# The queue of the first head's second load, and the place of one VectorE piece ahead of the first row maximum

## The chip, the cores and the metric

One core of a Trainium2 chip runs the whole program. The metric is the time that the device needs for one execution, in microseconds (us); of several runs the median counts.

## The reference

An attention with hashed buckets for 4 batches of 8 heads (768 tokens, 64 dimensions a head), followed by a mixture of 8 experts with one expert a token.

```python
q_bits = (np.einsum('bhsd,dk->bhsk', q, proj) > 0).astype(np.int64)
k_bits = (np.einsum('bhsd,dk->bhsk', k, proj) > 0).astype(np.int64)
powers = 2 ** np.arange(n_bits)
q_bucket = np.sum(q_bits * powers, axis=-1)
k_bucket = np.sum(k_bits * powers, axis=-1)
mask = q_bucket[:, :, :, None] == k_bucket[:, :, None, :]
scores = scale * np.matmul(q, k.transpose(0, 1, 3, 2))
scores = np.where(mask, scores, -1000000000.0)
scores = scores - np.max(scores, axis=-1, keepdims=True)
attn = np.exp(scores)
attn = attn / (np.sum(attn, axis=-1, keepdims=True) + 1e-09)
return np.matmul(attn, v).astype(np.float32)
...
for e in range(E):
    lo, hi = (boundaries[e], boundaries[e + 1])
    if lo == hi:
        continue
    h = np.maximum(x_sorted[lo:hi] @ w1[e], 0.0)
    y_sorted[lo:hi] = h @ w2[e]
y = y_sorted[inv_perm]
return (gate_w[:, None] * y).astype(np.float32)
```

## The kernel before

The 32 heads go in 16 pairs. A head's scores are made in units of 128 queries by 768 keys (12 units a pair), each in one of three PSUM buffers: two matmuls of the rounded halves of q and k (L309) and two of what rounding left, together with rows that hold the hash bits as large numbers (L307), so that keys of another bucket fall out in the exponent. VectorE takes a unit's row extreme and copies the unit to SBUF (L319, `peak`, called the maximum here), ScalarE takes the exponent (L325), and TensorE transposes (L339) and multiplies by v. Later pairs are transposed on VectorE and by DMA; the mixture of experts follows from about the middle of the run.

The order of the work on all engines is written out by hand. HEAD, a list of words, holds the first pair's order; `step` turns each word into instructions, and every engine executes its own in the order of the list. A word's first letter is the step, then come a head and a half (of 384 tokens), and a last letter names the engine (A ScalarE, V VectorE, P GpSimd). For the first pair:

- `load_first(h)` (L72 to L77) loads head h: the k half of the tile (columns S to 2S) first, then the q half, 384 KB each, both issued on SyncE (L76). L89 loads pj, the 16 KB of hash directions, on ScalarE's queue.
- k, j, q, l and p (`cut`, L219 to L236) make the parts of `qk` from the loaded tile `xd`: k and q round (L232 on ScalarE, L234 and L236 elsewhere), j takes what k's rounding left (L228, VectorE, needs k of the same half and the k load), l the same for q (L230), p copies q (L232, L236).
- y (L242) multiplies the loaded tile by pj; y01 takes the k load, y00 the q load. y11 and y10 are those of the second head.
- b (`bits_first`) turns y's result into bits: halves 0 and 1 on VectorE (L253), 2 and 3 on ScalarE (L247). b12 and b13 write over rows that j10V and j11V wrote.
- i are warming matmuls (L104), as are ten at the start.
- f0 and f1 are the two parts of the scores of unit 0; S1, S2, S11 and so on the scores of those units, R0, R1 their maxima (L319), X0, X1 their exponents (L325).
- G multiplies the next pair's tile by pj (L264), in a PSUM buffer that b12 and b13 have read before; H takes the signs of it.

ScalarE's pieces from k01A on are k01A, q00A, p00A, b03, b02, k11A, k10A, p10A, q10A, b13, b12, X0. GpSimd's are p01P, q01P, l01P, p11P, q11P, l11P, l10P. VectorE's are shown below under the change.

Of the kernel before, what the change touches and what calls it, by code (L numbers as in the profile page):

```python
# [15 lines left out]
B, H, S, D = 4, 8, 768, 64  # L16
# [38 lines left out]
def lsh_attention_moe(ctx, tc, qk, qk2, v, proj, wg, w1, w1p, w2, w2p, out):  # L55
    nc = tc.nc
# [15 lines left out]
    def load_first(h):  # L72

        x = wk.tile([128, 2 * S], F32, name="xd")
        for c in ((S, 2 * S), (0, S)):
            nc.sync.dma_start(x[:, c[0]:c[1]], qk2[h][:, c[0]:c[1]])  # L76
        XD[h] = x  # L77

    def load_pair(g):
# [3 lines left out]
    def load_v(g):  # L83
        VT[g] = wk.tile([128, NT, 2, D], F32, name="vt", bufs=3)
        nc.sync.dma_start(VT[g], v[g])

    load_first(0)
    pj = const.tile([128, 32], F32, name="pj")
    nc.scalar.dma_start(pj, proj)  # L89
    load_first(1)  # L90
    small = const.tile([128, 1], F32, name="small")
    nc.gpsimd.memset(small, -TINY)
# [928 lines left out]
    def weight_half(op, x):  # L1021
# [18 lines left out]
    lows = []  # L1040

    HEAD = """
        k01A k00V j00V y01 q00A j01V p00A y00 l00V b03 b00 i02 f0 p01P b02 q01P b01 k11A i12 f1 k10A j11V y11 R0 j10V
        y10 p10A q10A b13 l01P b12 S1 X0 p11P b11 b10 S2 G H R1 X1 R2 X2 q11P l11P S11 R11 X11 S10 R10 X10 l10P S4 T01
        E01v T00 E00v S5 T02 E02a S9 T51 E51a R5 X5 R4 X4 T50 E50v T52 E52a R9 X9 S3 R3 X3 S8 T20 E20v T21 E21v s01 w
        S7 T22 E22a R8 T10 E10a X8 A1 R7 X7 S6 s11 s13 s03 T11 E11v T12 E12v T41 z0 E41v R6 T40 e E40a T42 E42v z1 A2 s00
# [309 lines left out]
```

## Time and profile before

| | us |
|---|---|
| median of 3 runs | 679.37 |
| lowest and highest run | 679.32, 1693.6 |
| profiled execution | 679.44 |
| its span, first to last instruction | 677.7 |

The granted clock of TensorE is 1.0 of full speed in the profiled execution. In the rows of the profile PE is TensorE's matmuls, PEld its weight loads, DVE VectorE, ACT ScalarE, POOL GpSimd, SP SyncE; a q behind the name (SPq, ACTq) is the engine's sequencer, which issues DMAs. L76 is line 76 of the kernel.

### The profile page before, as it was taken

What the parts mean: (1) busy time and instruction counts of PE and PEld (TensorE: products, weight loads), DVE (VectorE), ACT (ScalarE), POOL (GpSimd) and SP (SyncE); (2) the same over time, 40 slices, a digit from 0 to 9 for tenths busy, and PEclk for the clock granted to TensorE, in tenths of its full rate; (3) what the DMA queues carried; (4) which work ended last, traced back from release to release, by engine and by line L of the source; (5) the groups of instructions that cost most, each with busy time, mean ns of one, the idle gap of its engine ahead of it and who ended that gap; (6) DMA issues with size and microseconds to landing.
All of it is one profiled execution on the core that took longest, in us unless ns stands there. A gap on an engine that the chain in (4) does not pass through costs nothing.

```text
span 677.7 us, 12615 instructions
## 1 busy us (share of the span) xinstructions
PE 666.5 (98%) x4359; PEld 564.1 (83%) x4359; DVE 471.2 (70%) x879; ACT 409.7 (60%) x816; POOL 468.0 (69%) x524
## 2 busy tenths in 40 slices
PE   8999999999999999999999999999999999999997
PEld 4777887788777887787777878899999999989896
DVE  8999889988899889998985555351453635463661
ACT  7977887788878887787765225453444444434310
POOL 7878666977797778877864636845476685959622
PEclk9999999999999999999999999999999999999999
DMA  7689999899889788997885358656648484857202
GB/s 278 210 248 291 254 264 278 211 255 238 228 238 263 197 239 238 261 246 192 242 250 162 116 199 243 158 183 159 168 150 218 147 214 145 227 190 226 96 10 43
DMA packets 74321, 138.51 MB, mean 204 GB/s; under 512 B 16609, under 2 KB 37345, under 8 KB 74256
## 3 DMA queue, kind: packets, MB, share of 16 engines
q1 hardware_dynamic: 66528, 118.57, 61.7%
q0 software_dynamic: 7584, 19.10, 9.5%
q8 instruction: 35, 0.57, 0.4%
q14 instruction: 30, 0.25, 0.2%
q10 hardware_dynamic: 144, 0.02, 0.0%
HBM read 63.39 MB, written 26.33 MB: 132 GB/s over the span
## 4 chain that ended last, share of the span: by engine, by line
PE 93%; ACT 2%; DVE 2%; issue 1%; DMA 1%; SPq 0%; POOL 0%; POOLq 0%; ACTq 0%; DVEq 0%
PE s L888 22%; PE t L415 12%; PE s L927 11%; PE s L961 10%; PE s L307 10%; PE s L309 9%; PE t L429 7%; PE t L339 7%; PE t L470 3%; PE t L264 2%; PE t L104 1%; ACT e L325 1%; DMA pt<-w 1%; ACT qk L215 0%; SPq L383 0%
## 5 line engine op out<-in xcount | busy, mean ns | idle before, releaser
L325 ACT ACTIVATE e<-e,m 128x768 f32<-128x768 f32 x192 | 178.3, 930 | 37.5 <-DVE e L319 36.0
L319 DVE TENSOR_SCALAR_CACHE_REDUCE e<-s 128x768 f32<-128x768 f32 x192 | 176.3, 951 | 25.3 <-PE s L309 20.2
L784 POOL TENSOR_TENSOR w<-raw,w 128x512 fp32r<-128x512 f32 x112 | 142.4, 1299 | 33.2 <-ACT w L783 32.3
L888 PE MATMUL s<-xh,w 128*128 128x456 f32 (+6 forms) x672 | 123.9, 345 | 0.0
L888 PEld LDWEIGHTS s<-xh,w 128*128 128x128 f32 x672 | 120.0, 188 | 3.1
L904 DVE SCALAR_TENSOR_TENSOR hh<-s,hh 128x256 fp32r<-128x256 f32 (+7 forms) x64 | 35.5, 555 | 86.8 <-ACT hh L902 86.7
L376 DVE STREAM_TRANSPOSE z<-e 128x1536 f32<-128x1536 f32 x52 | 90.7, 1763 | 2.3 <-DMA pt<-z 1.2
L415 PE MATMUL t<-pt,vt 128*64 128x256 f32 x720 | 81.0, 381 | 0.0
L902 ACT ACTIVATE hh<-s 128x256 fp32r<-128x256 f32 (+7 forms) x64 | 31.4, 491 | 80.8 <-PE s L888 80.8
L927 PE MATMUL s<-hh,w 128*128 128x456 f32 (+3 forms) x384 | 74.7, 355 | 0.0
L927 PEld LDWEIGHTS s<-hh,w 128*128 128x128 f32 x384 | 71.3, 188 | 2.7
L415 PEld LDWEIGHTS t<-pt,vt 128*64 128x64 f32 x720 | 50.4, 137 | 27.6 <-issue 3.1
L339 PE MATMUL t<-ident,e 128*128 128x128 f32 x468 | 68.9, 277 | 2.8 <-DVE pt L404 1.7
L339 PEld LDWEIGHTS t<-ident,e 128*128 128x128 f32 x468 | 53.3, 140 | 20.7 <-ACT pq L406 6.9
L783 ACT ACTIVATE w<-raw 128x512 fp32r<-128x512 f32 x112 | 66.3, 622 | 3.4 <-DMA raw<-in_w1p_dram 3.1
L961 PE MATMUL s<-w,hh 128*128 128x512 f32 (+1 forms) x240 | 56.4, 394 | 0.0
L406 ACT ACTIVATE pq<-t 128x512 f32<-128x512 f32 x83 | 47.8, 591 | 11.6 <-PE t L339 9.9
L307 PE MATMUL s<-w 80*128 80x384 f32 x192 | 54.1, 363 | 0.0
L307 PE MATMUL s<-qk 80*128 80x384 f32 x192 | 53.7, 361 | 0.0
L961 PEld LDWEIGHTS s<-w,hh 128*128 128x128 f32 (+1 forms) x240 | 44.7, 187 | 10.6
L309 PE MATMUL s<-qk 128*128 128x384 f32 x192 | 50.0, 341 | 0.0
L309 PE MATMUL s<-w 128*128 128x384 f32 x192 | 49.7, 340 | 0.0
(236 smaller groups left out, 1046.4 us busy)
## 6 DMA issues: line engine op xcount, KB each, us to landing
pt<-z SPq DMA_DIRECT2D x208, 192.0 KB
raw<-in_w1p_dram SPq DMA_DIRECT2D x28, 512.0 KB
xd<-in_qk_dram SPq DMA_DIRECT2D x14, 768.0 KB
sorted_rows<-xr SPq DMA_DIRECT2D x8, 1156.0 KB
raw<-in_w_dram SPq DMA_DIRECT2D x18, 512.0 KB
raw<-in_w2p_dram SPq DMA_DIRECT2D x16, 512.0 KB
vt<-in_v_dram SPq DMA_DIRECT2D x16, 384.0 KB
masks<-bits POOLq DMA_DIRECT2D x14, 192.0 KB
```

Source lines behind the costliest of these rows:

```text
L307: nc.tensor.matmul(p[:, a, :HALF], k[0:80, 2, c], k[0:80, 3, n], start=i >= 4, stop=i < 4)
L309: nc.tensor.matmul(p[:, a, :HALF], k[:, 0, c], k[:, 1, n], start=i < 4, stop=i >= 4)
L319: nc.vector.tensor_scalar(e, SC.pop(i)[:, :, :HALF], CEIL, None, op0=OP.min, op1=OP.min, accum_out=m)
L325: nc.scalar.activation(e, e, AF.Exp, bias=m, scale=-1.0, accum_out=SM[g][:, 3 * hf + t, s:s + 1])
L339: nc.tensor.transpose(o[:, j, w], e[w][:, kt // 3, (kt % 3) * 128:(kt % 3) * 128 + 128], ident)
L376: nc.vector.transpose(z[:, :, o].rearrange("p g (k i) -> p g k i", i=32), e)
L415: nc.tensor.matmul(PV[u][s * 64:(s + 1) * 64].rearrange("p (t b a i) -> p a t b i", t=4, b=2, a=2)[:, h], VT[g][:, kt, s, :], PT[u][:, h:: ...
L783: nc.scalar.activation(w[:, 0, a], r, AF.Copy)
L784: nc.gpsimd.tensor_tensor(w[:, 1, a], r, w[:, 0, a], op=OP.subtract)
L888: nc.tensor.matmul(p[:, :c], w[:, a, d, fs], x[:, b, d, :c], start=(k == 0), stop=(k == 11))
L927: nc.tensor.matmul(p[:, :c], w[:, a, f % 4, ms], h[b][:, f, :c], start=(k == 0), stop=(k == 23))
L961: nc.tensor.matmul(p[:pw], HH[n][b][:, f, i:i + pw], w[:, a, f % 4], start=(k == 0), stop=(k == 23))
```

## The change

Two edits. In `load_first` the second load (the q half) of head 0 is issued on ScalarE's queue; since `load_first(0)` stands ahead of the load of pj, it comes ahead of pj there. And in HEAD the word j10V stands in front of R0.

```diff
@@ -72,8 +72,8 @@
     def load_first(h):
 
         x = wk.tile([128, 2 * S], F32, name="xd")
-        for c in ((S, 2 * S), (0, S)):
-            nc.sync.dma_start(x[:, c[0]:c[1]], qk2[h][:, c[0]:c[1]])
+        for c, q in ((S, nc.sync), (0, nc.sync if h else nc.scalar)):
+            q.dma_start(x[:, c:c + S], qk2[h][:, c:c + S])
         XD[h] = x
...
     HEAD = """
-        k01A k00V j00V y01 q00A j01V p00A y00 l00V b03 b00 i02 f0 p01P b02 q01P b01 k11A i12 f1 k10A j11V y11 R0 j10V
+        k01A k00V j00V y01 q00A j01V p00A y00 l00V b03 b00 i02 f0 p01P b02 q01P b01 k11A i12 f1 k10A j11V y11 j10V R0
```

On VectorE, from l00V (L230) on, before (the two L253 rows are b00, b01 and b11, b10; L228 is j11V, then j10V; L319 is R0, then R1 and three more):

```order
L230 TENSOR_TENSOR qk<-xd,qk 64x384
L253 TENSOR_SCALAR qk<-t,thr,mul 16x384 x2
L228 SCALAR_TENSOR_TENSOR qk<-xd,qk 80x384
L319 TENSOR_SCALAR e,m<-s 128x768
L228 SCALAR_TENSOR_TENSOR qk<-xd,qk 80x384
L253 TENSOR_SCALAR qk<-t,thr,mul 16x384 x2
L319 TENSOR_SCALAR e,m<-s 128x768 x4
```

The same place now:

```order
L230 TENSOR_TENSOR qk<-xd,qk 64x384
L253 TENSOR_SCALAR qk<-t,thr,mul 16x384 x2
L228 SCALAR_TENSOR_TENSOR qk<-xd,qk 80x384 x2
L319 TENSOR_SCALAR e,m<-s 128x768
L253 TENSOR_SCALAR qk<-t,thr,mul 16x384 x2
L319 TENSOR_SCALAR e,m<-s 128x768 x4
```

j11V and j10V follow each other, and R0 comes behind both; the rest of VectorE's order is as it was.

On ScalarE, at its start, now (before, the row of L76 was not there and pj's stood first):

```order
L76 DMA xd<-in_qk_dram 128x768
L89 DMA pj<-in_proj_dram 128x32
L97 ACT_TABLE_LOAD
L97 ACTIVATE warm<-warm 1x1
L232 ACTIVATE qk<-xd 128x384 x2
L232 ACTIVATE qk<-xd 80x384
```

One issue more stands ahead of pj's. SyncE's row of L76 has three issues where it had four, and all behind it is unchanged, as are TensorE's and GpSimd's orders.

## Rows read from the trace of the kernel before

**Rows 1.** The page: TensorE's busy time, and the chain's shares by engine.

```profile
PE 666.5 (98%) x4359; PEld 564.1 (83%) x4359; DVE 471.2 (70%) x879; ACT 409.7 (60%) x816; POOL 468.0 (69%) x524
...
PE 93%; ACT 2%; DVE 2%; issue 1%; DMA 1%; SPq 0%; POOL 0%; POOLq 0%; ACTq 0%; DVEq 0%
```

**Rows 2.** The chain in order of time (start, length, what), and TensorE's timeline at S2.

```profile
5.38 0.79 PE t L242 x6
...
9.55 1.33 DVE qk L228
...
11.53 0.85 PE t L264 x8
...
10.19 0.52 PE L307 MATMUL s<-qk 80*128 80x384 f32 x2
```

**Rows 3.** Timeline of VectorE: start, length, line, operation, [idle before <-releaser].

```profile
4.52 1.02 DVE L228 SCALAR_TENSOR_TENSOR qk<-xd,qk 80x384 fp32r<-80x384 f32 x2
...
6.40 1.37 DVE L253 TENSOR_SCALAR qk<-t,thr,mul 16x384 fp32r<-16x384 f32 x2
7.99 0.55 DVE L228 SCALAR_TENSOR_TENSOR qk<-xd,qk 80x384 fp32r<-80x384 f32 x1 [0.23 <-ACT qk L232]
8.58 0.96 DVE L319 TENSOR_SCALAR_CACHE_REDUCE e<-s 128x768 f32<-128x768 f32 x1
...
9.46 1.41 DVE L228 SCALAR_TENSOR_TENSOR qk<-xd,qk 80x384 fp32r<-80x384 f32 x1
10.90 1.36 DVE L253 TENSOR_SCALAR qk<-t,thr,mul 16x384 fp32r<-16x384 f32 x2
12.20 0.94 DVE L319 TENSOR_SCALAR_CACHE_REDUCE e<-s 128x768 f32<-128x768 f32 x1
```

**Rows 4.** Waits from 3.5 to 20 us: total, times, longest.

```profile
ACT qk L247 <- DVE qk L228: 1.1, 1, 1.1
...
ACT pq L406 <- PE t L339: 0.5, 1, 0.5
PEld s L307 <- DVE e L319: 0.5, 2, 0.2
```

**Rows 5.** Timeline of the first DMA issues, columns as in rows 3.

```profile
0.77 0.39 ACTq L89 DMA_DIRECT2D pj<-in_proj_dram  x1
0.77 1.84 SPq L76 DMA_DIRECT2D xd<-in_qk_dram  x4
```

**Rows 6.** Timeline of ScalarE and VectorE: their first pieces on the loads.

```profile
4.12 0.52 ACT L232 ACTIVATE qk<-xd 128x384 fp32r<-128x384 f32 x1 [1.43 <-DMA xd<-in_qk_dram]
4.12 0.36 DVE L234 TENSOR_SCALAR qk<-xd 128x384 fp32r<-128x384 f32 x1 [0.84 <-DMA xd<-in_qk_dram]
...
5.09 0.94 ACT L232 ACTIVATE qk<-xd 128x384 fp32r<-128x384 f32 x2 [0.45 <-DMA xd<-in_qk_dram]
...
6.25 1.16 ACT L247 ACTIVATE qk<-t,small 16x384 fp32r<-16x384 f32 x2 [0.22 <-PE t L242]
...
7.44 1.76 ACT L232 ACTIVATE qk<-xd 128x384 fp32r<-128x384 f32 x4
```

**Rows 7.** Two stretches: length, engines' busy time, PEclk, DMA share, GB/s.

```profile
1.50:3.50 2.00, 2.00 (x6) 0.72 (x5) 1.68 (x14) 1.18 (x2) 1.00 (x2) 1.00 0.60 200
3.50:4.50 1.00, 1.00 (x4) 0.32 (x3) 0.36 (x1) 0.38 (x1) 0.20 (x2) 1.00 1.01 402
```

**Rows 8.** DMA queues, whole run, then 1.5 to 2.8 us: packets, MB, share.

```profile
q10 hardware_dynamic: 144, 0.02, 0.0%
...
q1 hardware_dynamic: 34, 0.10, 31.0%
q10 hardware_dynamic: 99, 0.01, 5.7%
```

**Rows 9.** Timeline of GpSimd: the casts of the fourth load, and l11P.

```profile
8.25 1.11 POOL L236 CAST qk<-xd 80x384 fp32r<-80x384 f32 x2 [0.48 <-DMA xd<-in_qk_dram]
9.45 1.01 POOL L230 TENSOR_TENSOR qk<-xd,qk 64x384 fp32r<-64x384 f32 x1
```

## Prediction

> **What bounds the kernel now.** I read the page first. TensorE is busy 666.5 of 677.7 us, and the chain that ended last lies on it for 93% of the span [rows 1]. So the kernel is a row of matmuls in a fixed order, and anything that delays or advances TensorE near the start moves the end by as much, unless slack further on takes it up. The change touches only the first 13 us, so I followed the chain through those, in order of time [rows 2]. The reader is to see that there it is not TensorE alone: after the ten warming matmuls end at 5.39 it goes through the two small matmul groups of L242, a few ScalarE pieces, then VectorE to 10.88 (9.55 + 1.33), one ScalarE sign and the matmuls of L264 at 11.53. Behind it stand score groups on TensorE, but these go in VectorE's step: the waits of the stretch show weight loads of L307 that stood twice, 0.5 us in all, for VectorE's L319 [rows 4], that is, for a maximum to free a PSUM buffer. So what counts is the time at which VectorE begins the second maximum, R1: 12.20 [rows 3].
>
> VectorE itself has hardly a hole from 4.12 to there [rows 3]: k00V, j00V, j01V, l00V, b00, b01, then 0.23 us of waiting for ScalarE, j11V at 7.99, R0 at 8.58, j10V at 9.46, b11 and b10 from 10.90, R1 at 12.20. One piece stands out. The pieces of L228 are the same operation on 80 x 384 elements; j11V takes 0.55 us and j10V 1.41.
>
> **Part 1, the queue of the first head's second load.** Removed: one of four issues at L76 on SyncE, which take 1.84 us for four, 0.46 each. Added: one on ScalarE's queue, ahead of the 0.39 us issue of pj [rows 5]. ScalarE's start-up work moves back by about 0.46; it stood idle for 1.43 us in front of its first piece at 4.12 [rows 6], which hides that. The SyncE DMAs behind are issued 0.46 earlier, but their data wait in the same stream behind the first loads; the issue itself costs and saves nothing.
>
> What matters is the arrival. ScalarE's k01A and VectorE's k00V both start at 4.12, when the first load (the k half of head 0) is there; q00A starts at 5.09 when the second is there, about one load later [rows 6]. The DMA engines move 200 GB/s from 1.5 to 3.5 and 402 GB/s from 3.5 to 4.5 [rows 7], that is 400 KB by 3.5 and 802 KB by 4.5. The first load (128 x 768 x 4 bytes = 393 KB) and pj (16) are 409 KB, reached at 3.52, and the release came 0.60 later; with the second load it is 802 KB, reached at 4.50, released 0.59 later. After 3.5 the transfers are bound by the engines' rate (share 1.01), not by the issue. A second queue therefore brings no earlier second load; the question is only how the two queues share. The packets of pj, the one transfer on ScalarE's queue now, answer it in part: that queue, q10, carries 144 packets in the whole run, and from 1.5 to 2.8 us 99 of them moved while SyncE's q1 moved 34 [rows 8]. Neither queue waited for the other to drain. If they share so with two loads of equal packets, each gets half, both are moved at 786 KB, reached at 4.46, and both land near 5.05, the first perhaps a packet earlier. Bounds for the delay of the first load: 0 (served as now) and 0.97 (landing with the second, 5.09 - 4.12). I take 0.90, 5.02 for the first load, near the upper end, because the packet counts are the nearest row.
>
> The Trainium skill speaks against this part: the page "DMA: Bandwidth & Descriptors", section "Rules for kernel authors", says that spreading DMAs over several issuing engines brings no bandwidth, since they run on the same 16 DMA engines and interleave, and its section "Queues, rings and completion order" that each engine goes round its queues packet by packet. The packet counts of rows 8 agree with it. By the rule alone the sum takes the upper bound, without it the lower.
>
> pj now comes behind the second load in ScalarE's queue, so after about 4.46 + 0.6 = 5.06, beside packets of the third load; it landed early enough in the trace for L242 to start right behind the warming matmuls. I put it between 5.1 and 5.7 (0.60 for the last part, and up to 0.6 of sharing), so TensorE waits 0 to 0.3 us at L242. That is covered: b03 on ScalarE needs the first half of L242 (half of its 0.79 us [rows 2]) and also VectorE's j01V, which now ends at 4.52 + 1.02 = 5.54 [rows 3] and with the later load at 6.44. Only a pj after about 6.0 would cost anything.
>
> Now VectorE with the first load at 5.02: the pieces up to b01 ended at 7.77 and end at 8.67. The 0.23 us of waiting for k11A in front of j11V goes: on ScalarE k01A runs 5.02 to 5.54, q00A and p00A to 6.50, b03 and b02 (1.16) to 7.67, k11A to about 8.2, so it is ready. j11V starts at 8.69, 0.70 late. On TensorE f1, y11, y10, S1 and S2 move by no more than the 0.90 of the load. S2 ended at 10.71 [rows 2] and so ends at 11.6 at the latest, with S1 0.9 ahead of it, before R1 (12.0) and R2 need them.
>
> **Part 2, j10V ahead of R0.** Nothing is added; two neighbours on VectorE change places. j10V needs k10A (ScalarE's four pieces from 7.44 end at 9.20 in the trace [rows 6]; k10A is the second, done near 8.4, about 8.7 now) and so follows j11V at 8.69 + 0.57 = 9.26. R0 comes after it. The waiters are b12 on ScalarE, which stood 1.1 us waiting for j10V [rows 4], and behind it L264 on TensorE. b12 can now follow at about 10.1, so L264 starts when S2 has ended, about where it started before (11.53). TensorE waits for R1 after it, so what R1 gains is what counts.
>
> What could change is j10V's duration. In the trace it began at 9.46, and GpSimd's l11P (L230) ran 9.45 to 10.46 [rows 9]; 1.41 us is that 1.0 and 0.4 of its own. The other L228 pieces took 0.55, the first two of them together 1.02 [rows 3]. I read that as: j10V came second and waited. Bounds for j10V: 0.55 and 1.41. At 9.26 it comes before l11P's 9.45, so I take 0.55, with a margin of 0.19 us only. Then j10V to 9.83, R0 0.88 to 10.71, the two bits pieces with their gaps 1.30 (10.90 to 12.20) and 0.03, and R1 starts at 12.04. Against 12.20 that is 0.16 earlier: +0.70 from the load, -0.86 from j10V.
>
> The Trainium skill's page "SBUF — State Buffer", section "Who interferes with whom", has this as a rule: VectorE with two SBUF inputs and a GpSimd instruction that reads SBUF exclude each other, and the order of their start decides who blocks. The 1.41 and the 9.45 of rows 3 and 9 agree. By it j10V costs 0.55 if it starts first and up to 1.41 if not, the two bounds above.
>
> **The sum.** The profiled execution took 679.44 us, 1.74 around its span of 677.7; the median of the runs is 679.37 (the third run, 1693.6, is far off and moves no median). With TensorE in the chain for 93% and two DMA parts of it at 1% [rows 1], I carry the 0.16 whole: 679.44 - 0.16 = 679.28, and against the median 679.21. I say 679.2. A difference of 2% (13.6 us) is about what a measurement of this kernel can tell from no change, and the stretch that is touched, up to R1, is 12.2 us long in all.
>
> **Rivals.**
> A, slower: j10V meets l11P after all. Place: VectorE at 9.26, GpSimd at 9.45. It decides once j10V starts behind l11P, that is when the first load lands later than 5.21, or when the third and fourth loads, now issued earlier, let GpSimd's casts (waiting until 8.25 for the fourth [rows 9]) and so l11P start 0.2 earlier. The price is j10V back at 1.41: -0.16 + 0.86 = +0.70, 680.1 us. For it: the margin is thin, and l11P follows its cast within 0.1 us. Against: if j10V is first, l11P waits and nobody on the chain waits for l11P.
> B, the change does not share as I think, and the first load lands at 4.12 as before. Then j11V stands at 7.99, j10V runs 8.56 to 9.13 and R0 follows; the whole 0.86 stays: 678.5. For it: pj, of 16 KB, is no load of 393 KB, so equal sharing is inferred. Against: the counts of q1 and q10, and a rate that is full.
> C, it is taken up later: R1 moves by a tenth or two, but a ScalarE eviction behind it waits 0.5 us for TensorE's transposes [rows 4], a place that could take it up, so that no change is left: 679.4.
>
> **How the numbers follow.** Forecast (between -0.4 and +0.2) 0.45, A 0.27, B 0.18, C 0.10. The forecast's own range is 678.9 to 679.6. For 8 in 10 I need most of A and of B: 678.4 takes in B's centre, 680.3 A's with the upper load bound (+0.07). None of the cases comes near 13.6 us: 0.98 for within 2%, 0.01 for each side.
>
> **What would show it.** Right: VectorE's k00V starts near 5.0 beside q00A; VectorE has no wait in front of j11V; j10V takes 0.55 and starts before l11P; R1 starts near 12.0; ScalarE's wait for j10V is gone and L264 starts at 11.6 at the latest. Wrong: k00V still at 4.12 (then B); a j10V of over 1 us (then A); L242 starting after 6.1, which would mean that pj, not the load, sets the pace; or R1 as forecast and an end that does not follow it.

## The result, and the profile after

| | before | changed kernel |
|---|---|---|
| median, us | 678.85 (6 runs, 678.17 to 679.37 and one of 1693.6) | 683.11 (6 runs, 681.94 to 684.03) |
| profiled execution, us | 679.44 | 684.03 |
| its span, us | 677.7 | 682.3 |

The ratio is 1.0063, interval 1.0053 to 1.0074: the changed kernel is slower by 4.3 us, or 0.6%, small but beyond its interval. The prediction said 679.2, with a range up to 680.3.

The page after, its slices of the span at the lines for TensorE, its granted clock, and the DMA rate:

```profile
span 682.3 us, 12614 instructions
...
PE   8999999999999999999999999999999999999997
...
PEclk7999999999999999999999999999999999999999
```

Each digit is a fortieth, 17 us. The clock line is the surprise: 7 tenths in the first slice, where the kernel before had its full clock in every slice. The stretches from 5.0 to 8.6 and from 8.6 to 18.9 us say where (columns as in [rows 7]: length, engines' busy time and instructions, PEclk, DMA share, GB/s), here of the kernel before:

```profile
5.00:8.60 3.60, 3.60 (x25) 1.49 (x24) 3.12 (x7) 3.25 (x7) 2.90 (x4) 1.00 1.01 376
8.60:18.90 10.30, 9.37 (x62) 6.95 (x56) 9.99 (x20) 8.33 (x19) 9.31 (x10) 1.00 0.84 303
```

and of the changed kernel:

```profile
5.00:8.60 3.60, 1.95 (x12) 0.41 (x10) 3.12 (x4) 1.75 (x4) 3.17 (x5) 1.00 1.03 404
8.60:18.90 10.30, 9.99 (x36) 5.97 (x37) 6.87 (x14) 6.36 (x14) 4.35 (x6) 0.50 0.46 148
```

TensorE was busy 1.95 of 3.60 us instead of all of it, and then for 10.3 us ran at 1.2 GHz, half of its 2.4: in the same stretch it got through 36 matmuls instead of 62 while it looked as busy as before or busier. A busy share alone does not show this; the count of instructions beside it does.

What came late in front of that, from the timeline of the changed kernel (to be held against [rows 3, 6 and 9]):

```profile
5.28 1.12 POOL L236 CAST qk<-xd 80x384 fp32r<-80x384 f32 x2 [1.58 <-DMA xd<-in_qk_dram]
5.42 1.35 ACT L232 ACTIVATE qk<-xd 128x384 fp32r<-128x384 f32 x3 [2.24 <-DMA xd<-in_qk_dram]
5.42 0.62 DVE L234 TENSOR_SCALAR qk<-xd 128x384 fp32r<-128x384 f32 x1 [2.14 <-DMA xd<-in_qk_dram]
...
6.03 0.96 PE L242 MATMUL t<-xd,pj 64*32 64x384 f32 x8 [0.58 <-DMA pj<-in_proj_dram]
6.07 2.01 DVE L228 SCALAR_TENSOR_TENSOR qk<-xd,qk 80x384 fp32r<-80x384 f32 x2
6.49 1.18 POOL L230 TENSOR_TENSOR qk<-xd,qk 64x384 fp32r<-64x384 f32 x1
...
8.11 0.74 DVE L230 TENSOR_TENSOR qk<-xd,qk 64x384 fp32r<-64x384 f32 x1
...
8.91 1.01 PE L309 MATMUL s<-qk 128*128 128x384 f32 x2 [1.38 <-DVE qk L230]
```

The same pieces of GpSimd, VectorE and TensorE in the kernel before:

```profile
5.13 1.56 POOL L236 CAST qk<-xd 80x384 fp32r<-80x384 f32 x2 [1.43 <-DMA xd<-in_qk_dram]
...
5.65 0.67 DVE L230 TENSOR_TENSOR qk<-xd,qk 64x384 fp32r<-64x384 f32 x1
...
6.46 0.71 PE L309 MATMUL s<-qk 128*128 128x384 f32 x2
```

Four things can be read. The first load is there at 5.42 instead of 4.12, and the second, which GpSimd's cast waited for, at 5.28, ahead of it. pj holds TensorE at L242 until 6.03, a hole of 0.58 us. VectorE's k00V, j00V, j01V and l00V (L234, L228 twice, L230) end at 8.85 and so take 3.43 us; before they ran from 4.12 to 6.32, 2.20 us. And f0 (L309) starts at 8.91 instead of 6.46, behind a second hole of 1.38 us.

To carry this to the end, I use the start of the first 48 matmuls of L415 (first pair times v, at 40.74 us before), a point behind the whole head, from the chain of waits, before and after:

```profile
40.74 5.33 PE t L415 x48
```

```profile
45.53 5.33 PE t L415 x48
```

It is 4.79 later; the span is 4.6 longer.

### The profile page after: what moved, and what is told of

It reads as the page before. It is cut to its first block, busy times and chain, and to the rows that moved or that the text cites. A ratio compares the mean times of both kernels' runs of the same rounds, so it can differ in the third digit from the quotient of the medians.

```text
span 682.3 us, 12614 instructions
## 1 busy us (share of the span) xinstructions
PE 669.8 (98%) x4359; PEld 566.7 (83%) x4359; DVE 468.9 (69%) x879; ACT 409.5 (60%) x816; POOL 468.7 (69%) x524
## 4 chain that ended last, share of the span: by engine, by line
PE 82%; DMA 5%; POOL 5%; issue 2%; ACT 2%; DVE 2%; SPq 1%; POOLq 0%; DVEq 0%; ACTq 0%
PE s L888 17%; PE t L415 11%; PE s L927 11%; PE s L307 9%; PE s L309 9%; PE t L429 7%; PE s L961 7%; PE t L339 6%; PE t L470 2%; DMA raw<-in_w1p_dram 2%; POOL w L784 2%; PE t L264 2%; DMA xd<-in_qk_dram 1%; ACT e L325 1%; DMA sorted_rows<-xr,slot 1%
## 5 line engine op out<-in xcount | busy, mean ns | idle before, releaser
L319 DVE TENSOR_SCALAR_CACHE_REDUCE e<-s 128x768 f32<-128x768 f32 x192 | 176.3, 951 | 27.2 <-PE s L309 21.9
L415 PE MATMUL t<-pt,vt 128*64 128x256 f32 x720 | 81.0, 381 | 0.0
L415 PEld LDWEIGHTS t<-pt,vt 128*64 128x64 f32 x720 | 50.4, 137 | 27.6 <-issue 2.8
L307 PE MATMUL s<-qk 80*128 80x384 f32 x192 | 55.3, 370 | 0.0
L307 PE MATMUL s<-w 80*128 80x384 f32 x192 | 54.0, 362 | 0.0
L309 PE MATMUL s<-qk 128*128 128x384 f32 x192 | 51.4, 349 | 1.4 <-DVE qk L230 1.4
L309 PE MATMUL s<-w 128*128 128x384 f32 x192 | 49.7, 340 | 0.0
```

The source lines that it names most:

```text
L307: nc.tensor.matmul(p[:, a, :HALF], k[0:80, 2, c], k[0:80, 3, n], start=i >= 4, stop=i < 4)
L309: nc.tensor.matmul(p[:, a, :HALF], k[:, 0, c], k[:, 1, n], start=i < 4, stop=i >= 4)
L319: nc.vector.tensor_scalar(e, SC.pop(i)[:, :, :HALF], CEIL, None, op0=OP.min, op1=OP.min, accum_out=m)
L415: nc.tensor.matmul(PV[u][s * 64:(s + 1) * 64].rearrange("p (t b a i) -> p a t b i", t=4, b=2, a=2)[:, h], VT[g][:, kt, s, :], PT[u][:, h:: ...
```

## The experiments

My first theory: the shared first load, the late pj and VectorE's collisions delay f0, TensorE's holes lower its clock, and j10V's place is no part of the loss. The rivals: j10V's place, pj's lateness by itself, the delay by itself without the clock. The table has the results; "L415" is the point named above in the one profiled execution, and the ratio is to the kernel before on the same chip. Ten runs stand behind each median, but 4 behind "queue alone" and "VectorE held, three", 5 behind "late pj", 6 and 9 behind the changed kernel, 11 behind "j10V alone again". The two rows of j10V alone are one program and lie 1.25 us apart at L415, so a smaller difference there says little.

| run | median us (before) | ratio, interval | f0 starts | L415 |
|---|---|---|---|---|
| before | | | 6.46 | 40.74 |
| changed | 683.11 (678.85) | 1.0063, 1.0053 to 1.0074 | 8.91 | 45.53 |
| j10V alone | 678.87 (678.33) | 1.0009, 0.9997 to 1.0021 | 6.39 | 39.91 |
| queue alone | 683.10 (678.33) | 1.0067, 1.0040 to 1.0094 | 8.92 | 45.60 |
| pj first | 678.40 (678.33) | 1.0004, 0.9994 to 1.0013 | 7.53 | 40.73 |
| more warming | 679.41 (678.33) | 1.0034, 1.0013 to 1.0054 | 8.94 | 41.89 |
| j10V alone again | 678.17 (678.43) | 0.9992, 0.9981 to 1.0003 | 7.01 | 41.16 |
| pj ahead on SyncE | 679.28 (678.43) | 1.0015, 1.0006 to 1.0025 | 7.92 | 41.59 |
| GpSimd waits | 680.57 (678.43) | 1.0029, 1.0020 to 1.0038 | 7.46 | 42.25 |
| VectorE held, two | 679.85 (678.43) | 1.0021, 1.0012 to 1.0030 | 8.07 | 41.63 |
| late pj, held three | 684.63 (679.56) | 1.0071, 1.0052 to 1.0090 | 9.02 | 42.57 |
| VectorE held, three | 684.71 (679.56) | 1.0079, 1.0054 to 1.0104 | 9.23 | 45.77 |
| changed, again | 683.39 (679.56) | 1.0054, 1.0040 to 1.0068 | 8.87 | 41.77 |

**Each half of the change alone.** j10V in front of R0, with all loads on SyncE:

```diff
-... j11V y11 R0 j10V
+... j11V y11 j10V R0
```

> Only j10V ahead of R0; all four first loads on SyncE as before. Theory 1 (the loss comes from the load's queue): k00V stays at 4.12, j10V takes 0.55 instead of 1.41 and starts before l11P, R1 starts near 11.3 to 11.4 instead of 12.20, the clock stays at 1.0, and the time is 0.4 to 0.9 us below the kernel before. Rival (the loss comes from R0 standing later): f0's maximum ends later, R1 no earlier than 12.2, and the time is 1 us or more above the kernel before.

And the second load on ScalarE's queue alone, with R0 in front of j10V as before:

```diff
-        for c in ((S, 2 * S), (0, S)):
-            nc.sync.dma_start(x[:, c[0]:c[1]], qk2[h][:, c[0]:c[1]])
+        for c, q in ((S, nc.sync), (0, nc.sync if h else nc.scalar)):
+            q.dma_start(x[:, c:c + S], qk2[h][:, c:c + S])
```

> Only the second load on ScalarE's queue; R0 ahead of j10V as before. Theory 1: k00V near 5.4 and TensorE's hole in front of f0 as in the changed kernel, the clock falls to 0.5 from about 8.6 for some 10 us, and the time is 4 to 5 us above the kernel before. Rival (j10V's place causes it): within 1 us of the kernel before.

The queue alone gives the whole loss, 1.0067, with the same picture in the trace (three of its four runs took 683.08 to 684.18 us, the fourth 680.36). j10V alone gives none. In its profiled execution the swap did about what was expected of it, as VectorE's timeline shows:

```profile
7.84 1.33 DVE L228 SCALAR_TENSOR_TENSOR qk<-xd,qk 80x384 fp32r<-80x384 f32 x2
9.20 0.96 DVE L319 TENSOR_SCALAR_CACHE_REDUCE e<-s 128x768 f32<-128x768 f32 x1
...
11.49 0.94 DVE L319 TENSOR_SCALAR_CACHE_REDUCE e<-s 128x768 f32<-128x768 f32 x1
```

j11V and j10V take 1.33 us together instead of 0.55 + 1.41, R1 starts at 11.49 instead of 12.20, and L415 0.83 earlier. But the median does not follow it (1.0009), so I ran it again, with more runs.

> The kernel of the first experiment once more (only j10V ahead of R0), with more runs. If the early gain is real and lost later: the first group of 48 matmuls of L415 starts 0.7 to 1.0 us earlier than in the kernel before, and the median still lies within 0.7 us of that kernel, as the stretch from 305 to 352 us takes it up. If the early gain was the luck of that execution: that group starts at 40.6 or later.

In this execution L415 stood at 41.16, later than before, and VectorE shows why:

```profile
6.95 1.37 DVE L253 TENSOR_SCALAR qk<-t,thr,mul 16x384 fp32r<-16x384 f32 x2 [0.52 <-PE t L242]
8.61 1.99 DVE L228 SCALAR_TENSOR_TENSOR qk<-xd,qk 80x384 fp32r<-80x384 f32 x2 [0.29 <-ACT qk L232]
10.63 0.96 DVE L319 TENSOR_SCALAR_CACHE_REDUCE e<-s 128x768 f32<-128x768 f32 x1
```

b00 waited 0.52 us for TensorE's L242, which began at 5.54 here and at 4.72 in the other execution of the same program; so j10V came behind GpSimd's l11P (8.99) and the pair of pieces took 1.99 us. The early gain was the luck of one execution, in part at least. Ratios of 1.0009 and 0.9992: the swap is worth nothing that these runs can tell from zero.

**pj in front of the second load on ScalarE's queue**, otherwise the changed kernel:

```diff
-    load_first(0)
     pj = const.tile([128, 32], F32, name="pj")
     nc.scalar.dma_start(pj, proj)
+    load_first(0)
```

> The changed kernel with pj issued ahead of the second load on ScalarE's queue. If the shared first load is the cause (theory 1): pj lands before 5, L242 starts near 5.4 behind the warming matmuls, but k00V stays near 5.0 to 5.4, f0 near 8.5 to 8.9 as it waits for l00V on VectorE, and the time stays 2.5 to 4.5 us above the kernel before. If pj's late arrival is the cause: f0 near 7.3 or earlier, the clock stays at 1.0, and the time is within 1 us of the kernel before.

The time is that of the kernel before (1.0004), as the rival said, but the timeline of this run shows that more than pj moved:

```profile
4.13 0.36 DVE L234 TENSOR_SCALAR qk<-xd 128x384 fp32r<-128x384 f32 x1 [0.86 <-DMA xd<-in_qk_dram]
...
4.96 0.84 PE L242 MATMUL t<-xd,pj 64*32 64x384 f32 x4
...
6.08 0.94 ACT L232 ACTIVATE qk<-xd 128x384 fp32r<-128x384 f32 x2 [1.43 <-DMA xd<-in_qk_dram]
```

The first load is back at 4.13, as the second now starts behind pj and no longer beside it; the second is the one that comes late, at 6.08 instead of 5.09, as it shares with the third load on SyncE's queue: from 4.2 to 4.8 us, with the first load landed, that queue moved 42 packets and ScalarE's 37. In this pair of runs one issue of 0.39 us ahead decided which of the two loads suffered. This run therefore cannot separate pj from the load.

**pj on SyncE ahead of the first load**, with the second load alone on ScalarE's queue, separates them better:

```diff
-    load_first(0)
     pj = const.tile([128, 32], F32, name="pj")
-    nc.scalar.dma_start(pj, proj)
+    nc.sync.dma_start(pj, proj)
+    load_first(0)
```

> The changed kernel with pj issued on SyncE ahead of the first load; the second load alone on ScalarE's queue at once. If the sharing of the two loads is enough: pj is early, L242 starts near 5.45 instead of 6.03, but k00V stays near 5.4, f0 near 8.9, the clock falls, and the time is 4 to 5 us above the kernel before. If the late pj is needed for the loss: the clock stays at 1.0 and the time is within 1.5 us of the kernel before.

The timeline of this run, all engines:

```profile
4.27 0.95 POOL L236 CAST qk<-xd 80x384 fp32r<-80x384 f32 x2 [0.57 <-DMA xd<-in_qk_dram]
...
5.18 0.36 DVE L234 TENSOR_SCALAR qk<-xd 128x384 fp32r<-128x384 f32 x1 [1.91 <-DMA xd<-in_qk_dram]
...
5.47 0.96 PE L242 MATMUL t<-xd,pj 64*32 64x384 f32 x8
...
5.58 1.70 DVE L228 SCALAR_TENSOR_TENSOR qk<-xd,qk 80x384 fp32r<-80x384 f32 x2
...
7.31 0.56 DVE L230 TENSOR_TENSOR qk<-xd,qk 64x384 fp32r<-64x384 f32 x1
...
7.92 0.62 PE L309 MATMUL s<-qk 128*128 128x384 f32 x2 [0.95 <-DVE qk L230]
```

The first load still lands a microsecond late (5.18), and the second overtakes it, at 4.27. Not all of that is the sharing: the first load's own issue now stands behind pj's and starts at 1.24 instead of 0.77. L242 follows the warming matmuls without a hole, f0 comes at 7.92, and the time is only 0.85 us above the kernel before; none of 10 runs exceeds 681.3. Since GpSimd also started earlier here, the gain of 3.4 us against the changed kernel belongs to pj and to these collisions together.

**GpSimd held back**: in the changed kernel, one small copy in front of p01P that reads what l00V writes.

```diff
...
-            cut(op, int(x[0]), int(x[1]), x[2])
+            w == "p01P" and nc.gpsimd.tensor_copy(C["seen"][64:128], QK[0][64:128, 0, 0:1]); cut(op, int(x[0]), int(x[1]), x[2])
```

> The changed kernel with one small GpSimd copy in front of p01P that reads what l00V writes, so that GpSimd starts on the first head only behind VectorE's l00V. If the collisions of VectorE and GpSimd make half of the delay in front of f0: k00V to l00V take 2.2 us instead of 3.45, f0 starts near 7.6 instead of 8.91, the clock stays at 1.0, and the time is within 1.5 us of the kernel before. If the later load alone makes it: l00V still ends after 8.3, and the time stays 4 to 5 us above.

The timeline of VectorE in this run:

```profile
5.39 0.36 DVE L234 TENSOR_SCALAR qk<-xd 128x384 fp32r<-128x384 f32 x1 [2.12 <-DMA xd<-in_qk_dram]
5.79 1.02 DVE L228 SCALAR_TENSOR_TENSOR qk<-xd,qk 80x384 fp32r<-80x384 f32 x2
6.84 0.56 DVE L230 TENSOR_TENSOR qk<-xd,qk 64x384 fp32r<-64x384 f32 x1
...
11.40 1.36 DVE L253 TENSOR_SCALAR qk<-t,thr,mul 16x384 fp32r<-16x384 f32 x2 [0.48 <-POOL qk L236]
```

With the first load at 5.39, k00V to l00V take 2.01 us to 7.40 instead of 3.43: the 1.4 between are collisions with GpSimd, shown by taking them away. f0 starts at 7.46. The clock stayed at its upper level in this execution, and the time falls from 4.3 to 2.1 us above, not to the 1.5 expected, since GpSimd itself is now late (VectorE waits for its casts in front of b01 and b11).

**The clock by itself.** Eight instead of two warming matmuls in front of f0, in the changed kernel:

```diff
-... b00 i02 f0 ...
+... b00 i08 f0 ...
```

> The changed kernel with eight instead of two warming matmuls in front of f0, which fill TensorE's hole from 7.5 to 8.9 and delay nothing. If the lower clock is a cause of its own: it stays at 1.0, f0 still starts near 8.9, the matmuls behind run at 0.34 us instead of 0.5 to 0.64, and the time falls to 1 to 2.5 us above the kernel before. If the delay of the loads alone makes the loss: the time stays 4 to 5 us above it, whatever the clock.

f0 starts at 8.94, as late as in the changed kernel, but the clock stays up and L415 is at 41.89 instead of 45.53:

```profile
8.60:18.90 10.30, 10.16 (x63) 6.99 (x62) 9.89 (x22) 9.39 (x21) 7.82 (x9) 1.00 0.74 256
```

The median is 1.1 us above the kernel before. With f0 as late as ever, what the six matmuls took away is not the delay but what TensorE's idleness did to its clock. Two of the ten runs, 683.14 and 685.01, lie where the changed kernel does; no trace of those was taken.

Then I made the hole without touching the loads: the kernel before, with two, and in another run three, reductions of the loaded tile on VectorE in front of l00V, whose result nobody uses; and the three together with pj issued behind the third load.

```diff
...
-            cut(op, int(x[0]), int(x[1]), x[2])
+            w == "l00V" and [nc.vector.tensor_reduce(C["held"], XD[0][:, S:], axis=AX.X, op=OP.max) for _ in range(2)]; cut(op, int(x[0]), int(x[1]), x[2])
```

> The kernel before (all loads on SyncE, R0 ahead of j10V) with two reductions of the loaded tile on VectorE in front of l00V, some 0.8 us each, that nobody uses: f0 moves from 6.46 to about 8.1 and TensorE gets a hole of about 1.3 us in front of it, without any change of the loads. If TensorE's hole is what lowers the clock: it falls to 0.5 for some 10 us behind it, and the time is 3.5 to 5 us above the kernel before. If the hole only delays: the clock stays at 1.0 and the time is 1 to 2 us above it.

> The same with pj where it was in the kernel before: one hole, of about 2.4 us, in front of f0 near 9.0. If the two holes together are needed: the clock stays at 1.0 in most executions and the time is 2 to 3 us above the kernel before. If one hole as long as the two does the same: the clock falls to 0.5 and the time is 4 to 6 us above it.

> The kernel before, all loads on SyncE, with pj issued behind the third load (so that L242 starts near 6.1 and TensorE has a hole of some 0.6 us in front of it) and three unused reductions on VectorE in front of l00V (f0 near 9.0, a second hole of 1.0 to 1.5 us). If the two holes together lower the clock, whatever makes them: it falls to 0.5 near 8.6 for some 10 us, and the time is 4 to 6 us above the kernel before. If the second queue itself is needed: the clock stays at 1.0 and the time is 2 to 3 us above it.

Two reductions: a hole of 1.46 us in front of f0, the clock stayed up, and the time rose by 1.4 us only. The expectation that a hole like that is enough fell. Three reductions: +5.2 us. Behind f0 its profiled execution was at the lower clock, which the view of stretches does not say, and only the lengths of the matmuls do:

```profile
8.60:17.30 8.70, 8.07 (x30) 4.17 (x30) 7.07 (x13) 3.58 (x8) 4.01 (x4) 1.00 0.56 188
```

30 matmuls in 8.7 us, as in the changed kernel (31), with a PEclk of 1.00; the L307 matmuls took 522 ns at the median there, 522 in the changed kernel, and 342 at the full clock. But TensorE's timeline shows the lower clock in front of the hole too:

```profile
5.46 1.62 PE L242 MATMUL t<-xd,pj 64*32 64x384 f32 x8
...
9.23 1.01 PE L309 MATMUL s<-qk 128*128 128x384 f32 x2 [1.18 <-DVE qk L230]
```

L242 took 1.62 us where it took 0.96 in the changed kernel, and the hole, of 1.18 us, is shorter than that of two reductions, which left the clock up. So here the hole did not lower the clock: the clock had not risen since the start, though TensorE had matmuls without a hole from 1.09 to 8.06. The mean granted clock of this execution is 0.998; the other three runs have 0.989 to 0.994, so a lower stretch is on record in them, and no trace shows where.

The late pj with three reductions gives +5.1 us. Its profiled execution, its fastest at 680.95, had one hole and not the two that were meant, 2.12 us in front of L242 (L243 in this kernel), as pj held TensorE until 6.84; the clock was down for a short time only, from 7.1 to 10.5, by the same views:

```profile
6.84 1.47 PE L243 MATMUL t<-xd,pj 64*32 64x384 f32 x8 [2.12 <-DMA pj<-in_proj_dram]
```

```profile
5.00:8.60 3.60, 1.76 (x9) 0.43 (x10) 3.50 (x6) 1.40 (x3) 2.24 (x3) 0.80 1.00 383
8.60:18.90 10.30, 10.30 (x61) 6.82 (x59) 10.13 (x21) 9.00 (x19) 7.97 (x9) 0.90 0.65 223
```

So no second queue is needed for a loss of 5 us: a TensorE held up at this place brings it with all loads on SyncE. That it is the same loss is not shown: f0 starts 2.77 and 2.56 us late in the two traces, against 2.45 in the changed kernel, and one of them has a clock that rose late, the other one that fell for 3.4 us. What decides on the clock cannot be read off a single trace, as the next run shows.

**The changed kernel again**, the same program on the chip of the last two.

> The changed kernel once more, on the chip of the two above. Theory 1: k00V near 5.4, L242 near 6.0, f0 near 8.9, the clock at 0.5 from 8.6 on for some 10 us, 4 to 5 us above the kernel before. If the fallen clock was the accident of one execution: 1.0 throughout and 1 to 2.5 us above it.

The profiled execution was one of the exceptions, by the view of stretches:

```profile
5.00:8.60 3.60, 1.50 (x10) 0.41 (x10) 3.15 (x4) 1.80 (x4) 3.21 (x5) 1.00 1.02 416
8.60:18.90 10.30, 10.01 (x62) 7.08 (x63) 9.89 (x22) 9.39 (x21) 7.80 (x9) 1.00 0.72 251
```

TensorE was even less busy from 5.0 to 8.6 (1.50), all pieces from k00V to f0 stand within 0.1 us of where they stood (k00V 5.38, L242 5.96, f0 8.87; only the ten warming matmuls took 3.88 us instead of 4.36), and yet the clock stayed at 2.4 GHz: 62 matmuls from 8.6 to 18.9. This execution took 679.76 us, the median of the kernel before on that chip being 679.56. Of the 15 runs of this program 13 took 681.9 or more and two 679.8 and 680.8. It is the cleanest pair in the study: one program, with and without the fall. L415 stands here at

```profile
41.77 5.33 PE t L415 x48
```

and at 45.53 in the other execution, so the lower clock costs 3.76 us, and all else that the change does costs 1.03 (41.77 - 40.74). The six warming matmuls, which left f0 late and kept the clock up, gave nearly the same: 3.64 (45.53 - 41.89). The 1.03 is less than the 1.25 by which the two executions of j10V alone differ there.

Of the 13 long runs ten have a mean granted clock of 0.991 to 0.995, as a fall leaves it (0.992 in the traced one). Three (683.14, 683.39 and 684.27) have 0.998 to 1.000, like the two short ones. The execution with three reductions, whose clock rose late, shows such a mean with such a time; whether these three were of that kind no trace tells.

## Why the prediction was wrong

Against its steps, in order:

- **That the two queues share, and the first load loses by it:** right, and rival B (arrival as before) is out. The size was off: 5.42 instead of 5.02, +1.30 instead of +0.90. I had set the second load's old arrival as the upper bound, but both came later than that: the first at 5.42, the second at 5.28. Nor was the sharing equal throughout: in the changed kernel ScalarE's queue moved 41 packets from 1.5 to 2.8 us and SyncE's 18 (its DMA queues in that stretch, as in [rows 8]):

```profile
q10 hardware_dynamic: 41, 0.13, 50.0%
q1 hardware_dynamic: 18, 0.06, 10.6%
```

  and then, from 2.8 to 3.6 us, as many as SyncE's:

```profile
q1 hardware_dynamic: 44, 0.14, 47.3%
q10 hardware_dynamic: 44, 0.14, 43.2%
```

  The half that I took held only in this later stretch; that the start is not even stood in [rows 8], 99 packets of pj against 34. Why the loads came 0.37 and 0.23 later than the 5.05 of half shares stays open. The packet rule of the Trainium skill's page "DMA: Bandwidth & Descriptors" ("Queues, rings and completion order"), taken as equal turns, gives the 0.97 bound. The counts agree with equal turns from 2.8 to 3.6 us and not before, and the delay, 1.30, lies outside that bound.
- **pj between 5.1 and 5.7, covered to 6.0:** it held L242 until 6.03. That costs VectorE and ScalarE little, as worked out, but it opens a hole on TensorE, which I had priced at nothing because b03 waits for j01V anyway.
- **VectorE's pieces move as a block by 0.90:** wrong. The two loads now arrive together, so GpSimd starts p01P at 5.28 beside k00V instead of 1.01 us after it, and l01P (6.49) catches j01V. The block grows from 2.20 to 3.43 us, +1.23, a term that the sum did not have. I had seen this collision at j10V, put 0.86 us on it, and not asked whether the shift of the load made it elsewhere. The Trainium skill's page "SBUF — State Buffer" ("Who interferes with whom") has the rule that the port VectorE and GpSimd share is an exclusive lock and that the order of issue decides who blocks. The trace agrees: two L228 pieces took 2.01 us beside GpSimd and 1.02 with GpSimd held back.
- **j10V at 0.55 and rival A:** j11V and j10V took 1.00 us together in the changed kernel (10.19 to 11.19), so they did not meet l11P. A's condition was met (a first load later than 5.21), but the pieces came so late that l11P (9.31 to 10.31) was all but over; A named the right side and the wrong place. With the swap alone the meeting came in one of the two traced executions (R1 at 12.92; 11.49 in the other).
- **TensorE moves by no more than the 0.90 of the load:** this is the step that failed most. It treats TensorE as an engine that only waits. Idle for 0.58 and 1.38 us between 5.45 and 8.91, it fell in the traced execution to half its clock for 10 us, and 13 of 15 runs are long like it (681.9 or more). That is 3.76 of the 4.79 us, and no term, bound or rival of mine had it. f0 itself was 2.45 late, 1.30 of the load and 1.23 of collisions less 0.08 of a shorter step behind l00V.
- **The sum without the clock:** R1 in the execution at the full clock started at 13.47, 1.27 late where I had 0.16 early: 2.45 less what the swap and VectorE's waits gave back. L415 was 1.03 late.
- **The whole shift reaches the end:** right for this size, 4.79 at 40 us and 4.6 at the end. For shifts below 1 us these runs cannot tell: between 326 and 352 us the chain leaves TensorE for DMAs (of pt in the kernel before, of the sorted rows and GpSimd's pieces in the first run of the swap), and single runs of either kernel scatter over 2 us.

What stays open: how the executions in which the clock falls differ from those in which it does not, beyond the observation that the clock first rises at another moment; how many of the long runs had a clock that fell and how many one that rose late; and how the 3.4 us that an early pj saved divide between pj and GpSimd's earlier start. None of the kernels tried was faster than the kernel before beyond its interval.

## What to carry to other kernels

A wait of TensorE on the critical path can have two prices: its length, and what its clock does afterwards; look at the instruction count and the PEclk of the next ten microseconds, and keep the engine fed with warming matmuls where a load may come late (six more of them brought L415 forward by 3.64 us here, though two of ten runs stayed long). Two loads that are wanted one after the other had best be on one queue: on two queues each took from the other here, and the one needed first came last (5.42 behind 5.28); only with pj issued ahead of the second did two queues cost nothing (1.0004). When an arrival moves, go through every pair of engines that now starts together, not only the pair that the change names.

## What the runs showed of the hardware that was not expected

- The same head of the same program does not run the same in each execution. With all loads on SyncE, the ten warming matmuls from 1.09 us on took 3.63 us in one execution and 4.45 in another, and L242 began at 4.72 and 5.54; the clock rises at another moment. The first rows are of the swap alone, the second of its repetition, from the chain in order of time:

```profile
1.09 3.63 PE t L104 x10
4.72 1.38 PE t L242 x8
```

```profile
1.09 4.45 PE t L104 x10
5.54 1.31 PE t L242 x8
```

- A PEclk of 1.00 is no proof of the upper clock: with three reductions it stood at 1.00 while matmuls took 522 instead of 342 ns, and seven microseconds of matmuls on end (1.09 to 8.06) had not brought the rise.
- k00V, with one input from SBUF, took 0.62 instead of 0.36 us when a GpSimd cast had started 0.14 us earlier, and 0.36 again with GpSimd held back, so not only pieces with two inputs are held up.
